# Attention with block means of v: loading the means' blocks in halves and earlier, and summing the second batch's two steps later

## The chip, the cores and the metric

One core of a Trainium2 chip. The metric is the time of one execution on the device in microseconds (us). Three executions of the kernel before gave 515.78, 517.11 and 518.01 us; the median, 517.11, is what the changed kernel is compared with.

The core has TensorE (PE, with its weight loads PEld), VectorE (DVE), ScalarE (ACT), GpSimd (POOL) and SyncE (SP). Each works through its own instructions in order and waits on semaphores for the others. In this kernel every DMA is issued by SP, in one order, and all of them run on the same 16 DMA engines.

## The reference

```
block, window = (32, 16)
k_sum = k.reshape(B, H, nb, block, D).max(axis=3)
v_sum = v.reshape(B, H, nb, block, D).mean(axis=3)
scores_l = scale * q @ k.T                # kept where |i - j| < window
scores_s = scale * q @ k_sum.T + log(block)
a = softmax(concat[scores_l masked, scores_s])
x = a @ concat[v, v_sum]                  # B=2, H=8, S=768, D=64
h = x @ w_in;  y = (h * cos(h)) @ w_out   # 1536 tokens, 512 -> 2048 -> 512
h2 = y @ w_in2                            # 512 -> 1024
out = layernorm(h2 * softmax(h2)) * g_ln @ w_out2
```

## The kernel before

Attention comes first and takes up to some 118 us; then two feed-forward blocks follow, in which TensorE multiplies without a break. The change is in attention only.

**Pairs and steps.** Heads are worked in pairs, two heads side by side on 128 partitions: 8 pairs, pairs 0 to 3 for batch 0 and 4 to 7 for batch 1. A pair is worked in 3 groups of 256 queries, so there are 24 groups. A written-out loop of steps (L592) is a pipeline over groups. In step s, in this order: TensorE computes the scores of group s+1 (`emit_s`, sps), transposes the weights of group s-4 (`emit_t`, aps) and multiplies them with v (group s-5, `emit_av`, ops); ScalarE takes the exponential of group s-1 (L508); VectorE sums group s-2 (L512) and adds the mask and finds the maxima of group s (L500, `emit_max`), which frees the score bank of group s for group s+2 (two banks); GpSimd subtracts the maxima (L503) and normalises group s-2 (L521); ScalarE copies the transposed weights (`emit_at`) and the product (`emit_x`). As no engine goes out of order, a wait in one step holds the next step's work on that engine.

**Keys and queries of a pair** are loaded (`load_k`, `load_q`), copied into one tile of both heads (`pair_k` on VectorE, `pair_q` on ScalarE), transposed on TensorE (`emit_k`, `emit_q`: 12 transposes, L431), then the block maxima of the keys are found on VectorE (`emit_ksum`, L443) and ScalarE builds the keys of all windows and the scaled queries (`emit_kx`, `emit_qx`). In most pairs that is spread over the three steps of the pair before.

**Means of v.** A batch's v is loaded once more in blocks of 32 rows (`load_vb`, the tile vb: 96 partitions, one per pair and block, with both heads' 32 rows; four DMAs, one per pair, into 24 partitions each). `sum_v` sums head 0 on VectorE in one instruction (L405) and head 1 on GpSimd as a tree of five (L409, L412). `scale_v` divides on ScalarE (L417), and `place_vsum` writes a pair's means by DMA beside the rows of v that `load_v` fetched (the tile vt, three buffers). Batch 0's blocks are asked for before the loop, behind pair 2's keys and queries, and summed in step 1; batch 1's are asked for in step 5 and summed in step 8.

**First weights.** From step 9 on the loop also loads blocks of the first feed-forward's weights (`raw`, 512 KB), two ahead, and converts and splits them: ScalarE rewrites both halves of the 64-bit words (`rebias`, L162, L163), VectorE joins them (`finish`, L170), one step later ScalarE rounds (L185) and GpSimd takes the rest (L186). Step 10 converts the first block, step 11 the second, step 13 the third. x is split likewise in steps 7, 10, 13 and 16 (L202, L203).

Of the kernel before, what the change touches and what calls it, by code (L numbers as in the profile page):

```python
# [17 lines left out]
BLOCK = 32  # L18
# [15 lines left out]
def fused_kernel(  # L34
# [299 lines left out]
    def attention():  # L334
        st = ExitStack()
        with st:
# [18 lines left out]
            def load_q(n):  # L355
                q_t[n] = load_heads(q, n, "qt")
# [19 lines left out]

            def load_v(n):
                b, hp = divmod(n, NP)
                t = io.tile([P, NT, 2, D], F32, tag="vt", name="vt", bufs=3)
                for j in range(2):  # L380
                    o = v[b, 2 * hp + j].offset
                    nc.sync.dma_start(
                        out=t[0:WIN, 1:NT - 1, j, :],
                        in_=bass.AP(v.tensor, o + (QT - BAND) * D, [[D, WIN], [QT * D, NT - 2], [1, D]]),
                    )
                    nc.sync.dma_start(
                        out=t[0:WIN, 0:NT:NT - 1, j, :],
                        in_=bass.AP(v.tensor, o, [[D, WIN], [(S - WIN) * D, 2], [1, D]]),
                    )
                v_t[n] = t  # L390
# [1 line left out]
            vb_t, vm_t = {}, {}  # L392

            def load_vb(b):
                t = io.tile([NP * NS, 2, BLOCK, D], F32, tag="vb", name="vb", bufs=1)
                for hp in range(NP):
                    nc.sync.dma_start(  # L397
                        out=t[hp * NS:(hp + 1) * NS],
                        in_=v[b, 2 * hp:2 * hp + 2].rearrange("h (n j) d -> n h (j d)", j=BLOCK))
                vb_t[b] = t  # L400

            def sum_v(b):
                t = vb_t.pop(b)
                m = io.tile([NP * NS, 2, D], F32, tag="vm", name="vm")
                nc.vector.tensor_reduce(  # L405
                    out=m[:, 0, :], in_=t[:, 0].rearrange("p j d -> p d j"), op=ALU.add, axis=AX.X)
                n = BLOCK // 2
                while n > 1:
                    nc.gpsimd.tensor_tensor(  # L409
                        out=t[:, 1, 0:n], in0=t[:, 1, 0:n], in1=t[:, 1, n:2 * n], op=ALU.add)  # L410
                    n //= 2
                nc.gpsimd.tensor_tensor(out=m[:, 1, :], in0=t[:, 1, 0], in1=t[:, 1, 1], op=ALU.add)  # L412
                vm_t[b] = m

            def scale_v(b):
# [151 lines left out]
            nc.sync.dma_start(out=mask.rearrange("p t k -> p (t k)"), in_=c_mask)  # L567
            load_k(1)
            load_q(1)
            load_k(2)  # L570
            load_q(2)
            load_vb(0)
            load_v(0)
            nc.gpsimd.memset(small, 0.0)
            warm_up(7)
            pair_k(0)
# [15 lines left out]
            for step in range(NGR + LA):  # L592
                n, g = divmod(step, GPP)
                summed = LN <= step < NGR + LN
                ahead = n + 1 if g == 0 and n + 1 < NPAIR else 0

                warm_up(IDLE[g] if step < min(FILL) else 0)
                fill(step)
# [3 lines left out]
                    emit_t(step - LT)  # L602
                if step >= LA:
                    emit_av(step - LA)
                if g == 2 and n + 2 < NPAIR:
                    emit_k(n + 2)
                    emit_q(n + 2)

                weights.split()
                if LX <= step < NGR + LX:  # L610
# [23 lines left out]
                for c in range(KC):  # L634
                    if step == XS[c]:
                        xs_of[0, c] = split_x(0, c, xs_a)
                if g == 1 and n + 2 < NPAIR:
                    pair_k(n + 2)
                    pair_q(n + 2)

                if g == 1 and n + 3 < NPAIR:
                    load_k(n + 3)
                    load_q(n + 3)
                if step == 1:
# [3 lines left out]
                    place_vsum(0)  # L648
                if g == 1 and n + 1 < NPAIR:
                    load_v(n + 1)  # L650
                if g == 2 and n + 1 < NPAIR:
                    if n + 1 == NP:
                        scale_v(1)
                    place_vsum(n + 1)
                if step == 5:
                    load_vb(1)
                if step == 8:
                    sum_v(1)

    with tc.manual_schedule():  # L660

# [260 lines left out]
```

## Time and profile before

| | us |
|---|---|
| median of three executions | 517.11 |
| profiled execution, its own time | 517.66 |
| its span, first to last instruction | 515.8 |
| TensorE busy in the span | 480.3 |
| VectorE | 309.8 |
| ScalarE | 275.0 |
| GpSimd | 155.4 |

The profile is of one execution. Shares of busy time are means over stages: TensorE is busy for 93% of the span, but almost all of its idle time lies in the attention stage. So the stage is read by the timeline (instructions in order of time, each with the idle time of its engine before it and what ended that), the table of stretches and the chain of waits. The granted clock is a share of TensorE's full speed.

### The profile page before, as it was taken

The numbers are of one execution on the slowest core, as the hardware profiler recorded it, in microseconds if no ns is written. First come the engines' busy times: TensorE is split into PE (matmuls) and PEld (weight loads), VectorE is DVE, ScalarE is ACT, GpSimd is POOL, SyncE is SP. The second block draws the span as 40 slices with busy tenths as digits, with TensorE's granted clock in tenths as the row PEclk, the third lists the DMA queues.
The fourth block names the chain that finished last, engine by engine and source line by source line (L and its number), as shares of the span: only waits on it lengthen the run. The fifth ranks groups of instructions, "written<-read, shape, count | busy, mean of one in ns | idle before, by whom it ended". The sixth has DMA issues, their size and how long they took to land.

```text
span 515.8 us, 7574 instructions
## 1 busy us (share of the span) xinstructions
PE 480.3 (93%) x2818; PEld 393.1 (76%) x2818; DVE 309.8 (60%) x684; ACT 275.0 (53%) x504; POOL 155.4 (30%) x147
## 2 busy tenths in 40 slices
PE   7378679899999999999999999999999999999997
PEld 4266567677888888888888888888887888888887
DVE  2486888796444546465565655646577755665561
ACT  3356698864758666566565563787422223222221
POOL 0386889752423223222222230254103102110000
PEclk9859799999999999999999999999999999999999
DMA  8798976600132332322322321220000000000001
GB/s 245 163 221 197 273 209 194 179 4 0 43 122 83 92 113 82 110 95 81 116 89 88 117 83 38 85 83 1 1 0 22 20 22 20 22 20 22 35 26 43
DMA packets 44516, 44.57 MB, mean 86 GB/s; under 512 B 21440, under 2 KB 36416, under 8 KB 44096
## 3 DMA queue, kind: packets, MB, share of 16 engines
q1 hardware_dynamic: 44480, 44.09, 29.0%
q8 instruction: 22, 0.36, 0.3%
q14 instruction: 14, 0.11, 0.1%
HBM read 39.76 MB, written 3.15 MB: 83 GB/s over the span
## 4 chain that ended last, share of the span: by engine, by line
PE 74%; DMA 6%; DVE 6%; ACT 5%; POOL 4%; SPq 3%; issue 2%; POOLq 0%; DVEq 0%; ACTq 0%
PE y L275 25%; PE h L233 23%; PE o L799 12%; PE h L721 11%; DMA vb<-in_v_dram 5%; PE tp L769 2%; DMA qt<-in_q_dram 1%; POOL vb L409 1%; POOL sm L521 1%; POOL sm L503 1%; DMA raw<-in_moe_w_in_dram 1%; DVE vm L405 1%; SPq L397 1%; ACT raw L162 1%; SPq L423 1%
## 5 line engine op out<-in xcount | busy, mean ns | idle before, releaser
L233 PE MATMUL h<-xs,w 128*128 128x512 f32 x576 | 141.5, 392 | 1.1 <-ACT qx L475 1.1
L275 PE MATMUL y<-gs,w 128*128 128x512 f32 x576 | 138.2, 389 | 0.0
L275 PEld LDWEIGHTS y<-gs,w 128*128 128x128 f32 x576 | 108.0, 188 | 22.5
L233 PEld LDWEIGHTS h<-xs,w 128*128 128x128 f32 x576 | 107.1, 188 | 23.6 <-ACT qx L475 1.3
L186 POOL TENSOR_TENSOR w<-s,w 128x512 fp32r<-128x512 f32 x48 | 62.1, 1295 | 161.2 <-ACT w L185 139.8
L242 ACT ACTIVATE r<-h 128x512 int32<-128x512 f32 x48 | 28.6, 596 | 86.1 <-PE h L233 86.1
L247 DVE SCALAR_TENSOR_TENSOR r<-r,h 128x512 f32<-128x512 int32 x48 | 32.9, 686 | 67.1 <-ACT r L242 67.0
L799 PE MATMUL o<-w,ls 128*128 128x512 f32 (+1 forms) x312 | 67.8, 374 | 1.4 <-DVE ls L773 1.4
L721 PE MATMUL h<-w,xs 128*128 128x512 f32 x288 | 68.6, 393 | 0.0
L170 DVE SCALAR_TENSOR_TENSOR s<-raw 128x512 int32<-128x512 int32 x48 | 37.0, 770 | 48.0 <-ACT raw L163 40.6
L799 PEld LDWEIGHTS o<-w,ls 128*128 128x128 f32 x312 | 55.3, 188 | 12.1 <-DVE ls L773 1.9
L721 PEld LDWEIGHTS h<-w,xs 128*128 128x128 f32 x288 | 53.3, 188 | 10.7
L489 PE MATMUL sps<-kx,qx 64*64 64x120 f32 x384 | 28.2, 292 | 22.6 <-DVE ss L516 10.8
L738 ACT ACTIVATE e<-h,st 128x1024 f32<-128x1024 f32 (+1 forms) x13 | 13.6, 1050 | 64.3 <-DVE st L734 60.7
L489 PEld LDWEIGHTS sps<-kx,qx 64*64 64x64 f32 x384 | 22.3, 147 | 28.4 <-issue 12.8
L756 POOL TENSOR_TENSOR st<-st,mhalf 128x1 f32<-128x1 f32 x12 | 6.6, 550 | 118.1 <-DVE st L755 105.9
L203 POOL TENSOR_TENSOR xs<-X,xs 128x512 fp32r<-128x512 f32 x22 | 28.7, 1313 | 30.0 <-ACT xs L202 30.0
L252 ACT ACTIVATE r<-r,half_pi 128x512 f32<-128x512 f32 x48 | 34.4, 717 | 1.3 <-DVE r L247 1.3
L263 DVE TENSOR_TENSOR gs<-h,gs 128x512 fp32r<-128x512 f32 x48 | 32.6, 680 | 4.1 <-ACT gs L262 3.8
L257 DVE TENSOR_TENSOR h<-h,r 128x512 f32<-128x512 f32 x48 | 32.9, 685 | 0.4 <-ACT r L252 0.4
L163 ACT ACTIVATE raw<-raw 128x512 int32<-128x512 uint32 x48 | 31.9, 665 | 0.0
L162 ACT ACTIVATE raw<-raw 128x512 f32<-128x512 f32 x48 | 31.9, 664 | 0.0
(73 smaller groups left out, 547.2 us busy)
## 6 DMA issues: line engine op xcount, KB each, us to landing
raw<-in_moe_w_in_dram SPq DMA_DIRECT2D x24, 512.0 KB, 3.4
raw<-in_moe_w_out_dram SPq DMA_DIRECT2D x24, 512.0 KB, 4.4
vt<-in_v_dram SPq DMA_DIRECT2D x16, 240.0 KB, 6.5
kt<-in_k_dram SPq DMA_DIRECT2D x8, 384.0 KB, 7.5
qt<-in_q_dram SPq DMA_DIRECT2D x8, 384.0 KB, 7.3
vb<-in_v_dram SPq DMA_DIRECT2D x8, 384.0 KB
out_dram<-osb SPq DMA_DIRECT2D x11, 256.0 KB, 2.1
vt<-vm SPq DMA_DIRECT2D x8, 144.0 KB
```

The source lines that it names most:

```text
L162: nc.scalar.activation(out=hw, in_=hw, func=AF.Prelu, scale=REBIAS, alpha=NEGATIVE)
L170: nc.vector.scalar_tensor_tensor(out=self.f32[i], in0=t[:, :, 1], scalar=3, in1=t[:, :, 0], op0=ALU.logical_shift_left, op1=ALU.bitwise_or)
L186: nc.gpsimd.tensor_tensor(out=w[:, 1, :], in0=f, in1=as32(w[:, 0, :]), op=ALU.subtract)
L233: nc.tensor.matmul(h, lhsT=w[:, a, f * P:(f + 1) * P], rhs=xs_of[tb, c][:, b_, :], start=(m == 0), stop=(m == 3 * KC - 1))
L247: nc.vector.scalar_tensor_tensor(out=r, in0=r.bitcast(I32), scalar=TWO_PI, in1=h_of[step], op0=ALU.mult, op1=ALU.subtract)
L252: nc.scalar.activation(out=r, in_=r, func=AF.Sin, scale=-1.0, bias=half_pi)
L257: nc.vector.tensor_tensor(out=h, in0=h, in1=r, op=ALU.mult)
L263: nc.vector.tensor_tensor(out=gs[:, 1, :], in0=r, in1=as32(gs[:, 0, :]), op=ALU.subtract)
L275: nc.tensor.matmul(y[e], lhsT=w[:, a, e * P:(e + 1) * P], rhs=gs[:, b_, :], start=(f == 0 and i == 0), stop=(f == GF - 1 and i == 2))
L489: nc.tensor.matmul(sps[h, i, :], lhsT=qx[h, t * QT:(t + 1) * QT], rhs=kx[h, t, :], start=True, stop=True)
L721: nc.tensor.matmul(banks[n], lhsT=xs_of[NTB + t // TPB, c][:, a, t0:t0 + P], rhs=weights.done[w2i[c][n]][:, b_, :], start=(m == 0), stop=( ...
L799: nc.tensor.matmul(o, lhsT=ls_of[t][f // 4][:, a, s0:s0 + P], rhs=w[:, b_, cols], start=(f == 0 and i == 0), stop=(f == NF2 - 1 and i == 2))
```

## The change

Five edits, all in the attention stage.

- `load_vb` fetches a pair's blocks in two halves of 16 rows: eight DMAs of 192 KB in place of four of 384 KB, into the same 24 partitions per pair. In `sum_v` VectorE's sum goes over two axes in place of one, and the tree's first addition adds the halves; sizes and counts stay.
- Before the loop, batch 0's blocks and pair 0's v are asked for ahead of pair 2's keys and queries.
- Pair 2's copies go from step 1 to step 2, its transposes from step 2 to step 3, its block maxima, kx and qx from step 3 to step 4; pair 3's loads go from step 1 to step 2.
- Batch 1's sum goes from step 8 to step 10, its scaling and the first placing from step 11 to step 12.
- v has four buffers in place of three.

```
-                t = io.tile([P, NT, 2, D], F32, tag="vt", name="vt", bufs=3)
+                t = io.tile([P, NT, 2, D], F32, tag="vt", name="vt", bufs=4)
...
-                    nc.sync.dma_start(
-                        out=t[hp * NS:(hp + 1) * NS],
-                        in_=v[b, 2 * hp:2 * hp + 2].rearrange("h (n j) d -> n h (j d)", j=BLOCK))
+                    src = v[b, 2 * hp:2 * hp + 2].rearrange("h (n a j) d -> n h a (j d)", a=2, j=BLOCK // 2)
+                    for a in range(2):
+                        nc.sync.dma_start(
+                            out=t[hp * NS:(hp + 1) * NS, a].rearrange("n h j d -> n h (j d)"), in_=src[:, :, a])
...
-                    out=m[:, 0, :], in_=t[:, 0].rearrange("p j d -> p d j"), op=ALU.add, axis=AX.X)
+                    out=m[:, 0, :], in_=t[:, :, 0].rearrange("p a j d -> p d a j"), op=ALU.add, axis=AX.XY)
+                nc.gpsimd.tensor_tensor(out=t[:, 0, 1], in0=t[:, 0, 1], in1=t[:, 1, 1], op=ALU.add)
...
             load_q(1)
+            load_vb(0)
+            load_v(0)
             load_k(2)
             load_q(2)
-            load_vb(0)
-            load_v(0)
...
-                ahead = n + 1 if g == 0 and n + 1 < NPAIR else 0
+                ahead = n + 1 if g == int(n == 1) and n + 1 < NPAIR else 0
...
-                if g == 2 and n + 2 < NPAIR:
-                    emit_k(n + 2)
-                    emit_q(n + 2)
+                if step == 3 or g == 2 and 0 < n < NPAIR - 2:
+                    emit_k((step + 4) // GPP)
+                    emit_q((step + 4) // GPP)
...
-                if g == 1 and n + 2 < NPAIR:
+                if g == (1 if n else 2) and n + 2 < NPAIR:
                     pair_k(n + 2)
                     pair_q(n + 2)
...
-                if step == 8:
+                if step == 10:
                     sum_v(1)
+                if step == 12:
+                    scale_v(1)
+                    place_vsum(NP)
```

SP's row of DMAs before the loop and in its first steps, before (kt and qt are keys and queries, vb the blocks, vt the rows of v):

```order
L350 DMA kt<-in_k_dram 128x6x128
L350 DMA qt<-in_q_dram 128x6x128
L397 DMA vb<-in_v_dram 24x2x2048 x4
L382 DMA vt<-in_v_dram 96x10x64
L386 DMA vt<-in_v_dram 96x2x64
L382 DMA vt<-in_v_dram 96x10x64
L386 DMA vt<-in_v_dram 96x2x64
L350 DMA kt<-in_k_dram 128x6x128
L350 DMA qt<-in_q_dram 128x6x128
L382 DMA vt<-in_v_dram 96x10x64
```

and now:

```order
L399 DMA vb<-in_v_dram 24x2x1024 x8
L382 DMA vt<-in_v_dram 96x10x64
L386 DMA vt<-in_v_dram 96x2x64
L382 DMA vt<-in_v_dram 96x10x64
L386 DMA vt<-in_v_dram 96x2x64
L350 DMA kt<-in_k_dram 128x6x128
L350 DMA qt<-in_q_dram 128x6x128
L382 DMA vt<-in_v_dram 96x10x64
L386 DMA vt<-in_v_dram 96x2x64
L382 DMA vt<-in_v_dram 96x10x64
L386 DMA vt<-in_v_dram 96x2x64
L350 DMA kt<-in_k_dram 128x6x128
```

The eight half loads and v of pair 0 stand ahead of pair 2's kt and qt, and v of pair 1 ahead of pair 3's.

TensorE's row from the first scores (sps) on, with the transposes of keys and queries (qk), before:

```order
L431 MATMUL qk<-ident,qg 128x128 x6
L489 MATMUL sps<-kx,qx 64x120 x24
L431 MATMUL qk<-ident,kg 128x128 x6
L431 MATMUL qk<-ident,qg 128x128 x6
L489 MATMUL sps<-kx,qx 64x120 x16
L528 MATMUL aps<-ident,sm 120x128 x4
L489 MATMUL sps<-kx,qx 64x120 x8
L528 MATMUL aps<-ident,sm 120x128 x4
L546 MATMUL ops<-at,vt 64x64 x8
L431 MATMUL qk<-ident,kg 128x128 x6
```

and now:

```order
L434 MATMUL qk<-ident,qg 128x128 x6
L492 MATMUL sps<-kx,qx 64x120 x32
L434 MATMUL qk<-ident,kg 128x128 x6
L434 MATMUL qk<-ident,qg 128x128 x6
L492 MATMUL sps<-kx,qx 64x120 x8
L531 MATMUL aps<-ident,sm 120x128 x4
L492 MATMUL sps<-kx,qx 64x120 x8
L531 MATMUL aps<-ident,sm 120x128 x4
L549 MATMUL ops<-at,vt 64x64 x8
L434 MATMUL qk<-ident,kg 128x128 x6
```

Eight rows of scores are one group, so x24 are groups 1 to 3 and x32 groups 1 to 4: pair 2's transposes (the qk rows behind them) stand one group later.

GpSimd's row around batch 1's tree (vb, vm), with the splits of x (xs) and of the weights (w), before:

```order
L521 TENSOR_TENSOR sm<-sm,ss 128x480
L409 TENSOR_TENSOR vb<-vb 96x1024
L409 TENSOR_TENSOR vb<-vb 96x512
L409 TENSOR_TENSOR vb<-vb 96x256
L409 TENSOR_TENSOR vb<-vb 96x128
L412 TENSOR_TENSOR vm<-vb 96x64
L503 TENSOR_TENSOR sm<-sm,mx 128x480
L521 TENSOR_TENSOR sm<-sm,ss 128x480
L503 TENSOR_TENSOR sm<-sm,mx 128x480
L521 TENSOR_TENSOR sm<-sm,ss 128x480
L203 TENSOR_TENSOR xs<-X,xs 128x512
L186 TENSOR_TENSOR w<-s,w 128x512
```

and now:

```order
L524 TENSOR_TENSOR sm<-sm,ss 128x480
L506 TENSOR_TENSOR sm<-sm,mx 128x480
L524 TENSOR_TENSOR sm<-sm,ss 128x480
L203 TENSOR_TENSOR xs<-X,xs 128x512
L409 TENSOR_TENSOR vb<-vb 96x1024
L412 TENSOR_TENSOR vb<-vb 96x512
L412 TENSOR_TENSOR vb<-vb 96x256
L412 TENSOR_TENSOR vb<-vb 96x128
L415 TENSOR_TENSOR vm<-vb 96x64
L186 TENSOR_TENSOR w<-s,w 128x512
L506 TENSOR_TENSOR sm<-sm,mx 128x480
```

The tree stood in step 8; now it stands in step 10, behind that step's split of x and right ahead of the first split of weights, which the subtraction of step 11 (L506, L503 before) follows.

## Rows read from the trace of the kernel before

**Rows 1.** stretches: us, busy (count) of PE, PEld, DVE, ACT, POOL; clock, DMA share, GB/s

```profile
18.44:28.60 10.16, 0.00 (x1) 0.03 (x1) 5.10 (x12) 0.00 (x0) 4.79 (x4) 0.72 0.85 202
...
49.62:56.70 7.08, 0.00 (x0) 0.00 (x0) 5.91 (x12) 1.25 (x3) 5.10 (x5) 0.78 0.87 230
...
117.80:515.80 398.00, 393.51 (x1816) 326.90 (x1816) 226.13 (x376) 199.23 (x360) 82.06 (x70) 1.00 0.17 57
```

**Rows 2.** timeline, first stall: start us, us, engine, line, operation, names, shapes [idle before <-releaser]

```profile
23.46 3.63 DVE L405 TENSOR_REDUCE vm<-vb 96x64 f32<-96x2048 f32 x1 [7.64 <-DMA vb<-in_v_dram]
...
23.50 5.03 POOL L409 TENSOR_TENSOR vb<-vb 96x1024 f32<-96x1024 f32 x4 [6.83 <-DMA vb<-in_v_dram]
...
28.60 1.86 PE L489 MATMUL sps<-kx,qx 64*64 64x120 f32 x16 [10.16 <-DVE ss L516]
...
28.61 0.32 POOL L412 TENSOR_TENSOR vm<-vb 96x64 f32<-96x64 f32 x1
...
28.96 0.31 ACT L417 ACTIVATE vm<-vm 96x128 f32<-96x128 f32 x1 [11.37 <-POOL vm L412]
...
29.29 2.15 SPq L423 DMA_DIRECT2D vt<-vm  x2
```

**Rows 3.** the chain of work to 75 us: start us, us, what

```profile
10.68 12.66 DMA vb<-in_v_dram
...
39.23 11.37 DMA vb<-in_v_dram
```

**Rows 4.** timeline, second stall, the columns of rows 2

```profile
50.79 3.63 DVE L405 TENSOR_REDUCE vm<-vb 96x64 f32<-96x2048 f32 x1 [3.80 <-DMA vb<-in_v_dram]
...
53.65 1.64 SPq L138 DMA_DIRECT2D raw<-in_moe_w_in_dram  x3
...
56.70 1.86 PE L489 MATMUL sps<-kx,qx 64*64 64x120 f32 x16 [7.09 <-DVE mx L500]
```

**Rows 5.** DMA in stretches of 2 us, the columns of rows 1

```profile
8.00:10.00 2.00, 1.55 (x15) 0.96 (x14) 1.40 (x3) 1.17 (x3) 0.00 (x0) 1.00 1.13 333
...
14.00:16.00 2.00, 1.09 (x18) 0.89 (x18) 1.83 (x13) 2.00 (x5) 1.57 (x2) 1.00 0.87 160
...
40.00:42.00 2.00, 2.00 (x37) 1.60 (x36) 1.97 (x17) 1.54 (x3) 1.22 (x2) 1.00 0.81 164
```

**Rows 6.** timeline, steps 10 to 13, the columns of rows 2

```profile
58.53 0.69 ACT L162 ACTIVATE raw<-raw 128x512 f32<-128x512 f32 x1
...
59.80 0.69 DVE L170 SCALAR_TENSOR_TENSOR s<-raw 128x512 int32<-128x512 int32 x1 [1.06 <-ACT raw L163]
...
60.73 1.15 POOL L521 TENSOR_TENSOR sm<-sm,ss 128x480 f32<-128x480 f32 x1 [1.06 <-DVE ss L520]
...
63.08 1.28 POOL L186 TENSOR_TENSOR w<-s,w 128x512 fp32r<-128x512 f32 x1
...
64.32 0.98 POOL L503 TENSOR_TENSOR sm<-sm,mx 128x480 f32<-128x480 f32 x1
...
65.06 0.31 ACT L417 ACTIVATE vm<-vm 96x128 f32<-96x128 f32 x1
...
66.42 0.59 ACT L508 ACTIVATE sm<-sm 128x480 f32<-128x480 f32 x1
...
69.83 0.64 ACT L508 ACTIVATE sm<-sm 128x480 f32<-128x480 f32 x1
...
71.60 0.69 DVE L170 SCALAR_TENSOR_TENSOR s<-raw 128x512 int32<-128x512 int32 x1 [1.35 <-ACT raw L163]
```

**Rows 7.** page, part 6, DMA issues: count, KB each, median us to landing

```profile
raw<-in_moe_w_in_dram SPq DMA_DIRECT2D x24, 512.0 KB, 3.4
raw<-in_moe_w_out_dram SPq DMA_DIRECT2D x24, 512.0 KB, 4.4
```

**Rows 8.** what the DMA queue (SP) waited for: us in total, times, longest

```profile
SPq L382 <- PE ops L546: 20.9, 5, 6.6
```

**Rows 9.** timeline, the transposes of pair 3's keys, the columns of rows 2

```profile
37.29 0.87 PE L431 MATMUL qk<-ident,kg 128*128 128x128 f32 x6
```

More of the change, by code (lines that the diff above doesn't have):

```diff
@@ L394, in load_vb @@
             def load_vb(b):
-                t = io.tile([NP * NS, 2, BLOCK, D], F32, tag="vb", name="vb", bufs=1)
+                t = io.tile([NP * NS, 2, 2, BLOCK // 2, D], F32, tag="vb", name="vb", bufs=1)
                 for hp in range(NP):
-                    nc.sync.dma_start(
-                        out=t[hp * NS:(hp + 1) * NS],
-                        in_=v[b, 2 * hp:2 * hp + 2].rearrange("h (n j) d -> n h (j d)", j=BLOCK))
+                    src = v[b, 2 * hp:2 * hp + 2].rearrange("h (n a j) d -> n h a (j d)", a=2, j=BLOCK // 2)
+                    for a in range(2):
+                        nc.sync.dma_start(
+                            out=t[hp * NS:(hp + 1) * NS, a].rearrange("n h j d -> n h (j d)"), in_=src[:, :, a])
                 vb_t[b] = t
@@ L405, in sum_v @@
                 nc.vector.tensor_reduce(
-                    out=m[:, 0, :], in_=t[:, 0].rearrange("p j d -> p d j"), op=ALU.add, axis=AX.X)
-                n = BLOCK // 2
+                    out=m[:, 0, :], in_=t[:, :, 0].rearrange("p a j d -> p d a j"), op=ALU.add, axis=AX.XY)
+                nc.gpsimd.tensor_tensor(out=t[:, 0, 1], in0=t[:, 0, 1], in1=t[:, 1, 1], op=ALU.add)
+                n = BLOCK // 4
                 while n > 1:
                     nc.gpsimd.tensor_tensor(
-                        out=t[:, 1, 0:n], in0=t[:, 1, 0:n], in1=t[:, 1, n:2 * n], op=ALU.add)
+                        out=t[:, 0, 1, 0:n], in0=t[:, 0, 1, 0:n], in1=t[:, 0, 1, n:2 * n], op=ALU.add)
                     n //= 2
-                nc.gpsimd.tensor_tensor(out=m[:, 1, :], in0=t[:, 1, 0], in1=t[:, 1, 1], op=ALU.add)
+                nc.gpsimd.tensor_tensor(out=m[:, 1, :], in0=t[:, 0, 1, 0], in1=t[:, 0, 1, 1], op=ALU.add)
                 vm_t[b] = m
@@ L636, in attention @@
                         xs_of[0, c] = split_x(0, c, xs_a)
-                if g == 1 and n + 2 < NPAIR:
+                if g == (1 if n else 2) and n + 2 < NPAIR:
                     pair_k(n + 2)
                     pair_q(n + 2)
-                if g == 1 and n + 3 < NPAIR:
+                if g == (1 if n else 2) and n + 3 < NPAIR:
                     load_k(n + 3)
@@ L650, in attention @@
                     load_v(n + 1)
-                if g == 2 and n + 1 < NPAIR:
-                    if n + 1 == NP:
-                        scale_v(1)
+                if g == 2 and n + 1 < NPAIR and n + 1 != NP:
                     place_vsum(n + 1)
```

## The prediction

> **What bounds the kernel now.** I read the stretches first. From 117.80 us on TensorE is busy 393.51 of 398.00 us at the full clock [rows 1]; no edit touches that part, so it only moves with the end of the attention stage. In front of it lie two stretches in which TensorE does nothing: 10.16 us up to 28.60 and 7.08 us up to 56.70 [rows 1]. The timeline names the cause: in both, VectorE's sum of v's blocks (3.63 us, starting at 23.46 and 50.79) stands ahead of the maxima that free the score banks, and TensorE's scores start only after it [rows 2, 4]. The chain of waits says what that sum waited for: the four loads of vb, landed at 10.68 + 12.66 = 23.34 us, and those of the second batch, at 39.23 + 11.37 = 50.60 us [rows 3]. So what both stalls hang on is the stream of loads, and the question is what a load becomes late for when another goes ahead of it. Behind 56.70 the steps are a ring of ScalarE, VectorE and GpSimd work: exponentials, conversion of the first weights, normalising, splitting [rows 6]. A delay inside that ring goes on to the end.
>
> **What the trace says of vb's rate.** At 8 to 10 us, when keys and queries are loaded, the queue moves 333 GB/s; at 14 to 16 us, in vb's first loads, 160, and at 40 to 42, in the second ones, 164 [rows 5]. Four loads of 384 KB are 1.57 MB; at 160 GB/s that is 9.8 us. Does a load in halves move faster? The rows show no half block, so I bound it: not at all (9.8 us) or at the keys' rate (1.57 MB / 333 GB/s = 4.7 us). I take 9.8, because whole and half blocks go into the same 24 partitions per load, and both stretches of whole blocks show one rate whatever ran beside them.
> The Trainium skill ("SBUF — State Buffer", Door 1: The DMA port swizzle) says that the rate of a DMA goes by how many of the 16 ports its partitions reach, four neighbouring partitions to a port; 24 partitions reach 6 ports, and 6/16 of its 435 GB/s is 163 GB/s, an estimate from that page. The trace agrees with 160 and 164. By that rule halves change nothing, and the sum stays; without it vb would be 5.1 us shorter, the case of the first rival.
>
> **First batch's vb ahead of pair 2's k and q.** Two loads of 384 KB (786 KB) no longer stand ahead of it. At 333 GB/s that is 2.4 us; at the stall's mean of 202 GB/s [rows 1] it would be 3.9. I take 2.5, nearer to the first, since k and q move at the fast rate: landing at 20.8 in place of 23.34. Eight issues in place of four cost SyncE more time (three took 1.64 us [rows 4], so some 2.2 us for four more), hidden beside the 10 us of data that the queue then moves; without that cover it would be 2.2 us. VectorE's sum keeps its 2048 elements and 3.63 us, GpSimd's tree keeps its sizes, from 23.50 to 28.61 + 0.32, which is 5.43 us [rows 2].
>
> **Pair 2 a step later.** Its copies, its 12 transposes and the building of its keys (kx, qx) go behind the stall. Before, the transposes ran ahead of it, free. Now they stand between the scores on TensorE, and the scores of step 5 wait for keys that ScalarE builds in step 4, behind that step's copy of the transposed weights: the slack of one step is gone. I followed steps 2 to 6 with the durations of the trace: pair 3's transposes, at 37.29 before [rows 9], come out within half a microsecond of that, so what the first stall gives up the steps spend again. The sum below doesn't hang on it, since step 10 waits for its weights either way with some 4 us in hand. What remains of the 2.5 us is that the queue runs earlier: the first mean of v is scaled at 28.96 and placed from 29.29 [rows 2], now 2.5 us sooner, and all loads behind that with it. Two loads more (pair 3's) are now issued ahead of the placing, as the order above shows: 0 to 1.1 us, at 0.55 an issue.
>
> **Second batch's sum two steps later.** vb's second loads land at 50.60 - 2.5 = 48.1 or later; the sum stands at the end of step 10, and the wait of 3.80 us at step 8 is gone from its place. Steps 9 and 10 now run ahead of the sum, and what they need next is late: step 10 converts the first weight block. Its load, the first of three issued from 53.65 [rows 4], stands behind the second vb and v of pair 3 in the queue. Moved by 2.5 us less 0 to 1.1 it is issued at 51.2 to 52.3; I take 51.4, since SyncE then still waits for the scaled means most of that time. The two kinds of weight loads land 3.4 and 4.4 us after issue in the median [rows 7]: 54.6 to 56.7, taken as 55.3 (the middle, 3.9 after 51.4). Before, ScalarE read that block at 58.53 without waiting for it [rows 6]: vb's stall had covered the load. Now ScalarE waits for it, with the conversion on VectorE behind it, and the sum and the tree behind that.
> From there, on rows 6. Conversion on VectorE: 59.80 - 58.53 = 1.27 us after ScalarE's start, so 56.6 (before 59.80). GpSimd then normalises, splits x and splits the weight block until it subtracts step 11's maxima; 64.32 - 59.80 = 4.52 us after the conversion's start, now with the tree between: 56.6 + 4.52 + 5.43 = 66.55, 2.2 later than before. Step 11's exponential waits for that (0.98 us): 67.55 for 66.42, 1.1 later. To step 12's exponential ScalarE has 69.83 - 66.42 = 3.41 us, and now also the scaling of the means, 0.31, which stood a step earlier [rows 6]: 71.3, 1.45 later. The third block's conversion (71.60 before [rows 6]) follows it by the same 1.45. The tree also meets a conversion on VectorE that reads two SBUF inputs; either may wait for the other, 0 to 0.69 us (one conversion), taken as 0.3.
> Sum: +1.75 us, of which I take 1.7; from +0.7 (weights at 54.6, no clash) to +3.5 (56.7 and a full clash), and -0.7 where vb gains the 3.9 us above.
>
> **Four v buffers.** SyncE waited 20.9 us in 5 pieces for the product with v to give a buffer back [rows 8]. These waits end. The first of them, before pair 3's v, is followed by issues that wait on room in the queue behind vb anyway; the later ones load v for a pair two or more steps ahead. I cost it at nothing; with more gained, the weights come up to 1 us sooner, which is inside the range.
>
> **Rivals.** (a) Halves move at the keys' rate. Then both vb's are 5.1 us shorter, the weights land by 46, ahead of use. Step 8 is through on VectorE at 50.79 - 3.80 = 46.99 [rows 4]; steps 9 and 10 took from 54.42 (the sum's end) to 59.80, 5.38 us, so the conversion starts at 52.4. With 4.52 + 5.43 step 11's subtraction comes at 62.3, 2.0 earlier than before, its exponential 3.0 and step 12's 2.7 earlier. The first stall also ends 5.1 us sooner, of which I count half, since the steps spend some of it: -5.2, which gives 511.9. For it speaks only that it was not measured; against it one rate in both stretches.
> (b) Slower: the queue gains nothing beyond the two extra issues and the tree clashes. The point is the weight block landing at 56.2: there the end is 2.6 us later. At 56.7 and a full clash it is 3.5 later: 520.6. For it: 1.1 us of issues and the slower landing median of 4.4 us give just that. Against: the first kind of weight load, which this one is, has the median of 3.4.
> (c) The change does not bring vb earlier: each load waits for the completion of the load eight issues back (the order shows one of eight counters before each), so eight small pieces hang on pair 1's loads, and v and pair 2's keys on the pieces. If vb still lands at 23.34, the weights land at 53.65 + 3.9 = 57.6, and the end is 1.7 + 2.3 = 4.0 later: 521.1. Against it: pair 1's loads and those ahead of them are 1.96 MB, 6 us at 333 GB/s, so in by 10 us, while vb's last piece is only due to move near 19.
>
> **How the numbers follow.** The profiled execution took 517.66 us, 0.55 above the median of 517.11; 517.66 + 1.7 = 519.4, on the median's scale 518.8. Half a per cent is 2.6 us, about what a measurement can tell from no change. Chances: forecast (no change beyond 2.6 us) 0.52, (b) 0.27, (a) 0.13, (c) 0.05, and 0.03 for a gain between (a) and the forecast. Faster 0.16, same 0.52, slower 0.32. The range goes from 514.0 (all but the most of (a)) to 521.3 ((c) and most of (b)); the forecast's own is 517.8 to 520.4.
>
> **What would show it.** In the changed kernel's trace: vb's sum starts near 20.9 and TensorE's first gap is some 2.5 us shorter; VectorE no longer waits for vb at step 8; ScalarE waits for the first weight block at step 10, up to about 55, and TensorE has a gap there; GpSimd's tree runs from about 60 to 65 and step 11's exponential comes at 67 to 68. I am wrong if the weights are there before step 10 asks for them, if vb's rate is above 200 GB/s, or if steps 11 to 13 have slack that takes the tree in.

## The result and the profile after

The changed kernel took 521.88 us in the median of 4 executions (520.55 to 521.90), the kernel before, beside it, 516.97 (515.78 to 518.01): a ratio of 1.0089, with an interval of 1.0062 to 1.0116. It is slower by 4.9 us. The prediction said 518.8 and a range up to 521.3; the time lies above the range. Measured again later on one chip with other kernels it was 521.31 to 516.46, 1.0096 (1.0069 to 1.0124).

The profiled execution took 520.55 us, 2.9 above that of before (517.66). I read it in the order of the prediction. The stretches (the columns of rows 1) answer to rows 1 and 5: the first gap of TensorE is 8.44 us where it was 10.16, the part behind attention is as long as before, and half blocks move at 158 and 168 GB/s in the two stretches shown (in stretches of 2 us from 34 to 38 us, where other loads run among them, the queue moves 138 to 203).

```profile
16.13:24.57 8.44, 0.01 (x1) 0.03 (x1) 5.11 (x12) 0.77 (x2) 4.81 (x5) 0.73 0.97 237
121.38:518.70 397.32, 392.94 (x1804) 326.45 (x1800) 225.36 (x375) 199.27 (x360) 82.07 (x70) 1.00 0.17 58
...
37.00:39.00 2.00, 2.00 (x22) 1.54 (x21) 0.00 (x0) 0.98 (x3) 0.00 (x0) 0.50 0.76 158
38.00:40.00 2.00, 2.00 (x19) 1.88 (x16) 0.00 (x0) 1.02 (x3) 0.00 (x0) 0.50 0.80 168
```

The timeline of the first batch (start us, us, engine, line, operation, names, shapes, idle before) answers to rows 2 and 9. The sum starts 4.0 us sooner than before and the scores too (24.57 for 28.60), but pair 3's transposes, 37.29 before, come at 38.50, and VectorE waits 4.57 us for them. Many of TensorE's rows here are long: six transposes take 1.54 us, in [rows 9] 0.87. And the copy of pair 2's keys (L368), done ahead of the stall before (0.76 us at 15.07), now stands right behind it and takes 2.55 us beside GpSimd's work: step 3's maxima come 8.23 us behind the start of the sum (27.66 - 19.43), before 6.63 (30.09 - 23.46). First the copy in the kernel before, then the rows of the changed one:

```profile
15.07 0.76 DVE L368 COPY kg<-kt 128x768 f32<-128x768 f32 x1
```

```profile
19.43 3.63 DVE L407 TENSOR_REDUCE vm<-vb 96x64 f32<-96x2048 f32 x1 [5.11 <-DMA vt<-in_v_dram]
...
24.57 1.87 PE L492 MATMUL sps<-kx,qx 64*64 64x120 f32 x16 [8.44 <-DVE ss L519]
...
24.64 2.55 DVE L368 COPY kg<-kt 128x768 f32<-128x768 f32 x1
...
27.24 1.54 PE L434 MATMUL qk<-ident,kg 128*128 128x128 f32 x6 [0.80 <-DVE kg L368]
...
34.61 1.86 PE L492 MATMUL sps<-kx,qx 64*64 64x120 f32 x16 [2.89 <-ACT qx L478]
...
38.50 1.54 PE L434 MATMUL qk<-ident,kg 128*128 128x128 f32 x6
...
41.02 0.96 DVE L446 TENSOR_REDUCE ksum<-qk 128x24 f32<-128x768 f32 x1 [4.57 <-PE qk L434]
```

The timeline of steps 10 to 13 answers to rows 4 and 6. VectorE no longer waits for vb: the sum stands behind the conversion (L170), the tree behind step 10's split of x. The first weight block is asked for at 49.98 (L138), and ScalarE starts on it (L162) at 55.01, right behind an exponential that ends at 54.93. Step 11's subtraction comes at 66.54, its exponential at 67.55, step 12's at 71.18.

```profile
49.98 1.64 SPq L138 DMA_DIRECT2D raw<-in_moe_w_in_dram  x3
...
54.33 0.60 ACT L511 ACTIVATE sm<-sm 128x480 f32<-128x480 f32 x1
...
55.01 0.67 ACT L162 ACTIVATE raw<-raw 128x512 f32<-128x512 f32 x1
...
56.24 0.69 DVE L170 SCALAR_TENSOR_TENSOR s<-raw 128x512 int32<-128x512 int32 x1 [2.67 <-ACT raw L163]
...
57.38 3.82 DVE L407 TENSOR_REDUCE vm<-vb 96x64 f32<-96x2048 f32 x1
...
59.51 2.37 POOL L409 TENSOR_TENSOR vb<-vb 96x1024 f32<-96x1024 f32 x1
...
65.04 0.32 POOL L415 TENSOR_TENSOR vm<-vb 96x64 f32<-96x64 f32 x1
...
66.06 4.61 DVE L519 TENSOR_SCALAR ss<-ss 128x4 f32<-128x4 f32 x1
...
66.54 0.98 POOL L506 TENSOR_TENSOR sm<-sm,mx 128x480 f32<-128x480 f32 x1
...
67.55 0.60 ACT L511 ACTIVATE sm<-sm 128x480 f32<-128x480 f32 x1 [3.05 <-POOL sm L506]
...
71.18 0.61 ACT L511 ACTIVATE sm<-sm 128x480 f32<-128x480 f32 x1
...
72.92 0.99 DVE L170 SCALAR_TENSOR_TENSOR s<-raw 128x512 int32<-128x512 int32 x1 [0.61 <-ACT raw L163]
```

SP's wait for a v buffer, 20.9 us in [rows 8], is all but gone:

```profile
SPq L382 <- PE ops L549: 1.0, 2, 0.8
```

**Where the time went.** I followed each group's exponential through both traces. Step 9's comes 3.7 us sooner than before, step 11's 1.1 later and step 12's 1.35 (forecast 1.1 and 1.45), step 14's 1.61 later; step 15's is 3.00 later, and the rows behind it stay about that late. Between steps 14 and 15 another 1.4 us appear that the prediction did not have. In front of them stand two rows out of the ordinary: a small addition on VectorE (L519, four numbers a row) that takes 4.61 us and not 0.19, and a run of TensorE at half clock from 68 to 78 us, where the kernel before had the full one (the expectations below write 68.7 to 78.5; read again it is 67.8 to 78.0). The chain of waits in this trace names both: it runs over the addition, and over TensorE from 72.37 to 87.44. Rows of TensorE there, the first four 1.6 to 1.8 times as long as with the filler further down:

```profile
72.37 1.87 PE L492 MATMUL sps<-kx,qx 64*64 64x120 f32 x16 [1.45 <-DVE ss L519]
74.17 1.11 PE L531 MATMUL aps<-ident,sm 128*120 128x128 f32 x4
75.20 1.12 PE L549 MATMUL ops<-at,vt 120*64 120x64 f32 x16
76.26 1.54 PE L434 MATMUL qk<-ident,kg 128*128 128x128 f32 x6
...
78.40 0.94 PE L233 MATMUL h<-xs,w 128*128 128x512 f32 x3
```

So three questions went to the chip. Is it the later sum that costs, or the first batch's edits (theories A and B)? Is the jump behind step 14 the half clock or the blocked addition (C and D)? And what holds the conversion in step 10, from which all else follows (E to H)?

### The profile page after: what moved, and what is told of

It reads as the page before. It is cut to its first block, busy times and chain, and to the rows that moved or that the text cites. A ratio compares the mean times of both kernels' runs of the same rounds, so it can differ in the third digit from the quotient of the medians.

```text
span 518.7 us, 7588 instructions
## 1 busy us (share of the span) xinstructions
PE 484.0 (93%) x2818; PEld 396.3 (76%) x2818; DVE 315.3 (61%) x684; ACT 275.6 (53%) x504; POOL 155.6 (30%) x147
## 4 chain that ended last, share of the span: by engine, by line
PE 75%; DVE 9%; DMA 6%; SPq 4%; ACT 2%; issue 1%; POOL 1%; DVEq 0%; ACTq 0%
PE y L275 25%; PE h L233 24%; PE o L804 12%; PE h L726 11%; DMA vb<-in_v_dram 2%; DMA vt<-in_v_dram 2%; SPq L386 2%; PE tp L774 2%; DVE vm L407 1%; DVE ss L519 1%; DMA raw<-in_moe_w_in_dram 1%; PE sps L492 1%; DVE sm L503 1%; PE ops L549 1%; SPq L350 1%
## 5 line engine op out<-in xcount | busy, mean ns | idle before, releaser
L804 PE MATMUL o<-w,ls 128*128 128x512 f32 (+1 forms) x312 | 67.8, 374 | 1.4 <-DVE ls L778 1.4
L170 DVE SCALAR_TENSOR_TENSOR s<-raw 128x512 int32<-128x512 int32 x48 | 36.7, 764 | 48.6 <-ACT raw L163 41.6
L185 ACT ACTIVATE w<-s 128x512 fp32r<-128x512 f32 x48 | 30.1, 627 | 5.0 <-DVE s L170 4.8
L162 ACT ACTIVATE raw<-raw 128x512 f32<-128x512 f32 x48 | 31.9, 664 | 0.1
```

Source lines behind the costliest of these rows:

```text
L162: nc.scalar.activation(out=hw, in_=hw, func=AF.Prelu, scale=REBIAS, alpha=NEGATIVE)
L170: nc.vector.scalar_tensor_tensor(out=self.f32[i], in0=t[:, :, 1], scalar=3, in1=t[:, :, 0], op0=ALU.logical_shift_left, op1=ALU.bitwise_or)
L804: nc.tensor.matmul(o, lhsT=ls_of[t][f // 4][:, a, s0:s0 + P], rhs=w[:, b_, cols], start=(f == 0 and i == 0), stop=(f == NF2 - 1 and i == 2))
```

## Which edit costs

**The sum back in step 8**, all else of the change kept:

```
-                if step == 10:
+                if step == 8:
                     sum_v(1)
```

with scaling and first placing back in step 11.

> The changed kernel with batch 1's sum back in step 8 and its scaling and first placing back in step 11; halves, early loads, pair 2's move and four buffers stay. Theory A (the later sum is the whole loss): vb's second loads land at 47.1 as in the changed kernel, ahead of the 49.2 at which VectorE asks for them (46.99 + 2.2), so nothing waits; step 9's maxima come at about 54.1 (55.76 before), the first weights, landed by 55.0, are not waited for, and the end is 1.6 us earlier than before: 515.4, that is 6 us below the changed kernel. Theory B (the early loads and pair 2's later step lose as well, since step 6 came 2.2 us late): the end is not earlier than before: 517 to 519.

Measured: 516.90 us in the median, before 516.65, ratio 1.0002 (0.9983 to 1.0021). Its profiled execution, 515.99, is the fastest of its twelve. In it the sum starts without a wait to speak of, as A said, and the lag of step 15 is -1.62:

```profile
49.16 3.72 DVE L407 TENSOR_REDUCE vm<-vb 96x64 f32<-96x2048 f32 x1 [0.20 <-DMA qt<-in_q_dram]
```

By the median A's gain of 1.6 us is not there: halves, early loads, pair 2's move and the fourth buffer make no difference in sum. Theory B's time, 517, holds: something eats what the vanished wait gives (the stretch from vb's sum to step 6, below).

**The sum in step 10 alone**, in the kernel before (sum, scaling and placing as in the change's last piece, nothing else).

> The kernel before with only batch 1's sum in step 10, its scaling and first placing in step 12. Theory A: the first weights are issued only at 53.6 and land at 57.1, step 10's conversion starts at 58.4 and not at 59.8, the tree follows it on GpSimd, step 11's subtraction comes at 68.3 (64.32 before): slower than before by 3 to 4 us, 520 to 521. Theory B: the move alone costs under 1 us: 517 to 518.

Measured: 522.64 us, ratio 1.0105 (1.0076 to 1.0134): 6.0 us slower, more than A's 3 to 4. ScalarE waits 6.77 us for the weights, the conversion stands where it stood before (59.77 for 59.80), and the sum and the tree behind it push step 12's exponential to 74.69, 4.86 later than before:

```profile
58.55 0.65 ACT L162 ACTIVATE raw<-raw 128x512 f32<-128x512 f32 x1 [6.77 <-DMA raw<-in_moe_w_in_dram]
59.77 0.69 DVE L170 SCALAR_TENSOR_TENSOR s<-raw 128x512 int32<-128x512 int32 x1 [9.37 <-ACT raw L163]
...
63.04 5.44 POOL L409 TENSOR_TENSOR vb<-vb 96x1024 f32<-96x1024 f32 x4
...
74.69 0.60 ACT L508 ACTIVATE sm<-sm 128x480 f32<-128x480 f32 x1
```

So the move of the sum is the loss. The other edits make no difference by themselves; that they give back about 1 us of it (522.64 for 521.88 and 521.31) is not shown, as the intervals overlap.

**The sum in step 9**, one step later than before (the same edit with 9).

> The changed kernel with batch 1's sum in step 9, one step later than before and one earlier than in the change; scaling and first placing in step 11 as before. Theory E: VectorE sums and GpSimd runs the tree in the time in which step 10 waits for the weights anyway; the tree is over by 58.4, the conversion at 57.6 is not held, step 11's subtraction comes at 62.1 (64.32 before): 515 to 516, the best so far. If the sum costs its 3.63 and 5.43 us wherever it stands behind step 8, it is slower than before by 2 us or more: 519.

Measured: 517.70 us, ratio 1.0020 (1.0002 to 1.0039). That is 4.2 us below the changed kernel, between the two expectations: in step 9 the sum lies beside the wait for the weights for the most part. It is 0.8 above the sum in step 8, within the intervals, so it is not shown to be faster or slower than that. Its profiled execution is the slowest of twelve, so I take nothing finer from it.

## The jump behind step 14

**Filler on TensorE.** `warm_up(n)` multiplies a constant tile n times into a bank that nobody reads.

```
-                warm_up(IDLE[g] if step < min(FILL) else 0)
+                warm_up({12: 13, 13: 5, 14: 6}.get(step, 0))
...
                     emit_s(step + 1)
+                warm_up({13: 6}.get(step, 0))
```

> The changed kernel with idle products on TensorE (13 ahead of step 12's scores, 5 ahead of step 13's, 6 behind them, 6 ahead of step 14's; 0.21 us each), in the gaps of 59.5 to 72.4 us; no other work is touched. Theory C (the half clock from 68.7 to 78.5 costs: it stretches TensorE's run from step 14's scores on by 2.6 us): the clock stays full there and the end is 1.4 us earlier than in the changed kernel, since ScalarE's chain, 1.6 us behind the kernel before, then sets it. Theory D (only VectorE's small addition of 4.61 us at 66.06 costs): the clock stays full and the time is the changed kernel's, within 0.3 us.

Measured: 520.53 us (ratio 1.0067, 1.0041 to 1.0093), 1.35 below the changed kernel's 521.88 and 0.8 below its second median; the intervals overlap, so the trace has to decide. The granted clock from 66 to 76 us (the columns of rows 1, clock third from the end) is 0.59 in the changed kernel, the first line, and 1.00 with filler, the second:

```profile
66.00:76.00 10.00, 6.80 (x70) 5.47 (x72) 9.36 (x27) 8.45 (x18) 8.48 (x9) 0.59 0.30 82
```

```profile
66.00:76.00 10.00, 8.67 (x99) 5.26 (x97) 9.33 (x25) 6.03 (x13) 9.02 (x11) 1.00 0.17 58
```

The rows of TensorE that answer to those above, in the kernel with filler:

```profile
75.43 1.04 PE L492 MATMUL sps<-kx,qx 64*64 64x120 f32 x16 [0.95 <-DVE ss L519]
76.59 0.62 PE L531 MATMUL aps<-ident,sm 128*120 128x128 f32 x4
77.14 0.69 PE L549 MATMUL ops<-at,vt 120*64 120x64 f32 x16
77.76 0.88 PE L434 MATMUL qk<-ident,kg 128*128 128x128 f32 x6
...
79.04 0.94 PE L233 MATMUL h<-xs,w 128*128 128x512 f32 x3
```

From the scores to the product h it is 3.61 us (79.04 - 75.43) where the changed kernel takes 6.03. And the jump is gone: the lag to the kernel before is 4.68 us at step 14's exponential and 4.68 at step 15's. The addition still takes 4.62 us in this run. (That the lag is large in this profile comes from a conversion at 59.28; more on that below.)

**Without the addition** of 1e-9 in step 12:

```
-                if summed:
+                if summed and step - LN != 10:
                     emit_guard(step - LN)
```

> The changed kernel without one instruction: the addition of 1e-9 to group 10's sums in step 12 (the one that took 4.61 us at 66.06) is left out. Theory D: VectorE goes on at once, step 13's maxima come 2 to 4 us earlier than 71.33 and the end 1.4 us or more earlier. Theory C alone (half clock): the end moves by under 0.4 us. If both stand in series on TensorE, either this or the filler takes the 1.4 us, down to ScalarE's chain. If the reciprocal behind it is held in its place (4 us instead of 0.18), nothing moves and the addition itself was not at fault but the port it shares.

Measured: 521.52 us, ratio 1.0093 (1.0066 to 1.0120). VectorE does go on at once: step 13's maxima, 15.09 us behind the conversion in the changed kernel (71.33 - 56.24), come 12.52 behind it (70.09 - 57.57). Yet the clock is half, the rows of TensorE are as long as in the changed kernel, and the lag still jumps, from 2.66 us at step 14's exponential to 3.91 at step 15's:

```profile
70.09 0.27 DVE L503 CUSTOM_DVE_ANT_0 sm<-sps,mask 128x120 f32<-128x120 f32 x1
...
70.90 2.99 DVE L519 TENSOR_SCALAR ss<-ss 128x4 f32<-128x4 f32 x1
```

```profile
72.52 1.86 PE L492 MATMUL sps<-kx,qx 64*64 64x120 f32 x16 [0.27 <-ACT qx L478]
...
76.92 1.54 PE L434 MATMUL qk<-ident,kg 128*128 128x128 f32 x6
```

This run alone doesn't clear the addition, since part of the wait only moved: the same addition of the next step, at 70.90, now takes 2.99 us. But there it holds no row of TensorE: the scores at 72.52 wait for ScalarE's qx. And in the run with filler the addition takes its 4.62 us while the jump is gone. With the two together theory D falls, and so does "either of the two takes it": the most striking row of the trace, 4.61 us for four numbers and a piece of the chain of waits, costs nothing that these runs can see. The jump is the half clock (C).

## What holds the conversion

In eight profiles with the sum in step 10 I read the start of step 10's conversion (C) and of step 12's exponential. The distance is the same to 0.05 us in all of them, whatever else was changed, 4.9 us more than before:

| profiled execution | C | step 12's exponential | distance | time | time - C | half clock behind step 12 |
|---|---|---|---|---|---|---|
| before | 59.80 | 69.83 | 10.03 | 517.66 | 457.86 | no |
| the change | 56.24 | 71.18 | 14.94 | 520.55 | 464.31 | yes |
| the change again | 56.04 | 70.97 | 14.93 | 519.85 | 463.81 | yes |
| without the addition | 57.57 | 72.52 | 14.95 | 521.77 | 464.20 | yes |
| weights first | 57.18 | 72.12 | 14.94 | 521.00 | 463.82 | yes |
| sum in step 10 alone | 59.77 | 74.69 | 14.92 | 523.30 | 463.53 | yes |
| filler, steps 12 to 14 | 59.28 | 74.25 | 14.97 | 522.25 | 462.97 | no |
| filler everywhere | 56.64 | 71.61 | 14.97 | 519.62 | 462.98 | no |
| filler and weights first | 53.63 | 68.58 | 14.95 | 516.62 | 462.99 | no |

The time of an execution is C, plus 463.0, plus 0.5 to 1.3 us where TensorE runs at half clock behind step 12. The kernel before has 457.9 there: the sum behind the conversion costs 5.1 us and must be earned by a conversion that comes earlier. What keeps it from coming earlier?

**The first weight block asked for in step 5**, ahead of batch 1's blocks:

```
                 if step == 5:
+                    weights.load(0)
                     load_vb(1)
```

> The changed kernel with the load of the first weight block asked for in step 5, right ahead of batch 1's blocks, in place of step 9; nothing else is touched. In three profiles the conversion came 1.25 us after that block had landed (54.98, 56.32 and 58.03), and the end followed the conversion. Theory E (the landing sets the conversion): ScalarE is free at 54.9, the conversion comes at 56.2 in every run, and the median falls by 1.3 us from 521.9 to 520.6. Theory F (ScalarE and VectorE are not free sooner, the wait is only a resting place): no change, 521.5 to 522.

Measured: 521.34 us, ratio 1.0074 (1.0045 to 1.0103). The time doesn't decide: by the medians the gain is 0.5 us at most, by the ratios (1.0074 for 1.0089 and 1.0096) about 1, and the intervals overlap. The trace does, against E: the conversion is at 57.18 and not at 56.2. The weights are there long before, but ScalarE isn't: it starts on them where its exponential ends, at 56.0.

```profile
55.44 0.61 ACT L511 ACTIVATE sm<-sm 128x480 f32<-128x480 f32 x1
...
55.92 0.69 ACT L162 ACTIVATE raw<-raw 128x512 f32<-128x512 f32 x1
...
57.18 0.69 DVE L170 SCALAR_TENSOR_TENSOR s<-raw 128x512 int32<-128x512 int32 x1 [2.51 <-ACT raw L163]
```

So two floors lie under the conversion, both near 55 to 56: the weights' landing, and the steps themselves. That the steps are so late goes back to the first batch. From the start of vb's sum to step 6's maxima the kernel before takes 16.27 us (23.46 to 39.73), the changed one 22.47 (19.43 to 41.90), and what the sum wins is lost again there. TensorE ran at half clock in most of that stretch, and 1.6 us of the 6.2 stand at step 3's maxima already, behind the copy of 2.55 us.

**Filler in all gaps of TensorE**, and **the same with the weights first**: two runs that lift the second floor alone, and both.

```
+                warm_up({3: 33, 5: 10, 11: 8, 12: 13, 13: 5, 14: 6}.get(step, 0))
...
                     emit_s(step + 1)
+                warm_up({3: 6, 13: 6}.get(step, 0))
```

> The changed kernel (sum in step 10) with idle products on TensorE in all its gaps: 33 ahead of step 3's scores and 6 behind them, 10 ahead of step 5's, 8 ahead of step 11's, and those of the run with filler in steps 12 to 14. Theory G (two floors under step 10's conversion: the first weights' landing, 56.3 in a usual run, and ScalarE's own steps, free at 56.0 since pair 2's transposes ran at half clock): the filler lifts only the second; the landing still sets the conversion, so the time is that of the run with filler in steps 12 to 14: 520.5, above the kernel before by 3.5 to 4.5. Theory H (the late step 6 is what costs): 517 to 518.

Measured: 520.22 us, ratio 1.0086 (1.0058 to 1.0113). As G said: the steps are early now (vb's sum at 19.04, step 6's maxima at 37.45, 18.41 us behind it), the exponential is through at 50.5, and ScalarE waits 4.93 us for the weights.

```profile
49.88 0.62 ACT L511 ACTIVATE sm<-sm 128x480 f32<-128x480 f32 x1
55.42 0.65 ACT L162 ACTIVATE raw<-raw 128x512 f32<-128x512 f32 x1 [4.93 <-DMA raw<-in_moe_w_in_dram]
56.64 0.69 DVE L170 SCALAR_TENSOR_TENSOR s<-raw 128x512 int32<-128x512 int32 x1 [7.53 <-ACT raw L163]
```

> The same filler, and the first weight block asked for in step 5 as in the run with the weights first. Theory G: with both floors lifted the conversion comes at 52.5 to 53.5 and not at 57.2, and the end 3 to 4 us earlier than with the filler alone: 516.5 to 517.5, though the sum still stands in step 10. If the sum in step 10 costs its time in any case, 519.5 to 520.5.

Measured: 515.51 us, ratio 0.9983 (0.9965 to 1.0001), 1 us below the range that G gave. With both floors lifted the conversion is at 53.63 in a profile whose first loads were late (vb's sum at 21.06), and the kernel with the sum in step 10 is 4.7 us faster than with filler alone and 5.8 faster than with the weights first alone. Either floor alone hides what the other is worth.

```profile
52.37 0.68 ACT L162 ACTIVATE raw<-raw 128x512 f32<-128x512 f32 x1
...
53.63 0.69 DVE L170 SCALAR_TENSOR_TENSOR s<-raw 128x512 int32<-128x512 int32 x1 [2.51 <-ACT raw L163]
```

**Filler with the sum in step 9, and in the kernel before.** Four counts in the first case (`{3: 33, 5: 10, 11: 12}` ahead of the scores, `{3: 6}` behind), two in the second (`{3: 40, 10: 28}`).

> The kernel of the sum in step 9 with idle products on TensorE in the first gap (33 ahead of step 3's scores, 6 behind them), ahead of step 5's scores (10) and of step 11's (12). Theory C: TensorE is at full clock from 20 to 41 us, pair 2's transposes take 0.9 in place of 1.5 us and step 6 comes 1 to 1.5 us sooner; the end gains that only if the sum, not the weights, sets step 10: 0 to 1.2 us below the kernel without filler. If the clock there costs nothing, the same time within 0.3 us.

Measured: 515.86 us, ratio 0.9976 (0.9955 to 0.9998), against 1.0020 (1.0002 to 1.0039) without filler; the gain of 1.8 us is above the 0 to 1.2 expected. The clock from 18 to 41 us is 1.00 (first line), without filler 0.65 from 18 to 42 (second):

```profile
18.00:41.00 23.00, 20.90 (x209) 13.57 (x206) 19.58 (x72) 10.60 (x20) 15.55 (x16) 1.00 0.99 244
```

```profile
18.00:42.00 24.00, 11.90 (x95) 9.58 (x92) 15.37 (x49) 8.08 (x15) 13.11 (x13) 0.65 0.90 222
```

> The kernel before with idle products on TensorE in its two gaps (40 ahead of step 3's scores, 28 ahead of step 10's). Theory C: the clock stays full from 23 to 37 and from 54 to 61 us, but behind both gaps GpSimd, ScalarE and the loads set the pace, not TensorE: the time stays within 0.5 us of 516.7. If the half clock costs wherever it falls, as it does behind step 13 of the changed kernel, the time falls by 1.3 us or more.

Measured: 517.01 us, ratio 1.0001 (0.9984 to 1.0018): no difference, as C expected. From vb's sum to step 6's maxima filler takes 2.3 us off the kernel before too (13.99 for 16.27), but there step 8 waits for vb's second loads, and most of the time won ends in that wait (5.53 us for 3.80). Behind the second gap the filler did not hold the clock (0.73 from 54.6 to 61 us), so the run tests the first gap alone. In these runs the half clock costs only where TensorE's work is what the next step waits for.

**Sum in step 9, filler, weights first.**

> The kernel with the sum in step 9 and filler (515.9), and the first weight block asked for in step 5. There ScalarE waited 2.8 us for that block; GpSimd's tree, over at 54.1, stands beside that wait. Theory G: the conversion comes earlier, but the tree is then what step 10 waits for: 0.3 to 1.5 us less, 514.5 to 515.5. If vb's second loads, now behind the block, come too late for step 9, the time is not lower: 516 to 517.

Measured: 515.33 us, ratio 0.9994 (0.9968 to 1.0020), executions from 513.34 to 520.21. The spread is too wide to set it above or below the two kernels at 515.5 and 515.9. In its profiled execution, one of the slower ones (517.48), a load holds the sum of step 9, and the sum holds the conversion: ScalarE is on the weights at 52.46, but VectorE is in the sum until 55.95 and converts at 57.30. Whether that is so in the faster executions stays open.

```profile
52.16 3.79 DVE L407 TENSOR_REDUCE vm<-vb 96x64 f32<-96x2048 f32 x1 [2.78 <-DMA kt<-in_k_dram]
```

> The changed kernel itself, beside the others on one chip. It took 521.9 us in the median and 520.55 in the profiled execution. Every theory expects 521 to 522; its profile shows whether the conversion at 56.24 of the first profile was early (landing 54.98) against a usual run (56.3 expected, and conversion at 57.6).

Measured: 521.31 us, ratio 1.0096; its profiled execution, 519.85, has the conversion at 56.04, straight behind an exponential from 54.30: there the steps were the floor, and the weights' landing, that I expected to see, was not.

## Why the prediction failed

**Right.** Halves move at the old rate, 158 to 168 GB/s; rival (a) falls. The ring of steps 10 to 13 came out nearly as forecast: the conversion at 56.24 (forecast 56.6), step 11's subtraction at 66.54 (66.55), its exponential at 67.55 (67.55), step 12's at 71.18 (71.3), the third block's conversion 1.32 later than before (1.45). VectorE's wait in step 8 is gone. With four buffers SP's waits for one are all but gone, and no run shows a gain from it.

**In part luck.** That the ring's times are so near comes from misses that cancel. The first weight block was asked for at 49.98 and not at 51.4, and ScalarE read it 5.0 us after that and not 3.9. ScalarE hardly waited for it: its own steps were over at 54.93, so the conversion would have come at about 56.1 without any load (an estimate from the second profile of the changed kernel, where it comes at 56.04 behind an exponential from 54.30, here from 54.33). And from the conversion to step 11's subtraction it took 10.30 us for 9.95, which makes up for a conversion 0.36 earlier.

Two steps failed: what the earlier conversion earns was taken 1.7 to 2.2 us too high, and the clock of TensorE, 0.8 to 1.3 us, was left out. Together they are the 3.1 us between forecast and result.

**The step that failed: "Sum: +1.75 us", taken from step 12's exponential straight to the end.** The sum follows ScalarE, VectorE and GpSimd. TensorE is not in it: the prediction names its gap in step 10 as a sign, and doesn't ask at what clock TensorE comes back. Here it idled for 3.08 us up to 62.61 and 1.34 up to 66.19, and twice more behind, was granted half clock from 68 on, and its rows became the path. From step 14's exponential to step 15's that costs 1.4 us in the first profile of the changed kernel, 0.9 in the second, and nothing with filler.

**Mis-sized: what the earlier conversion earns, 3.2 us.** The prediction set one execution of the changed kernel against one of before. By the table an execution of before at the median, 516.97, would have its conversion at 59.1 (516.97 - 457.86), and one of the changed kernel at 521.88 at 57.6 or 58.1 (less 464.31 or 463.81, its two profiles): estimates, since no trace of such a pair exists. The gain is then 1.0 to 1.5 us. With the 5.1 for the sum behind it and 0.8 to 1.3 for the clock that is the +4.9 measured. That the profiled executions lay on opposite sides of their medians (before 0.7 above it, the change 1.3 below) made the two traces look nearer than the kernels are; the 0.55 that the prediction allowed for it was on one side only.

**"The sum doesn't hang on it", of pair 2's later step.** This was the reason given for not following steps 2 to 6 further, "with some 4 us in hand". There was nothing in hand. Pair 3's transposes came not within half a microsecond of 37.29 but 1.2 later, step 6's maxima 2.2 later, although vb's sum started 4.0 sooner and not 2.5. (In eleven profiles with the change's first loads it started between 19.04 and 21.51, 20.23 in the mean, in three with those of before between 21.83 and 23.46, 22.73 in the mean: 2.5 was right as a usual value, and the 4.0 comes from the two executions that were set side by side.) The steps reached the conversion at the same moment as the weights. The stretch from the sum to step 6's maxima grew by 6.2 us, 16.27 to 22.47. With filler it is 13.99 in the kernel before and 18.41 in the changed one: 4.4 of the 6.2 are pair 2's moved step and the order around it, and the half clock takes 4.1 in place of 2.3, which is the other 1.8. Of the 4.4, 1.6 stand at step 3's maxima, with filler or without, behind the copy of pair 2's keys that takes 2.55 us (2.47 with filler) beside GpSimd: the prediction moved that copy without asking which engine would be at work beside it. No run takes the copy out, so its share is argued. The clock is the same omission as above at another place: the scores behind the gap took 1.86 us in [rows 2], and I did not ask why.

**The clash, 0.3 us, at most 0.69.** The tree took 5.85 us for 5.43, 0.4 more. But a small addition waited 4.61 us, far beyond the bound, and that cost nothing that shows.

**Rival (b)** had the direction and, at its bound, 520.6, a time 1.3 short, by a mechanism that holds in part: in two of four profiles of the same first twelve steps the weights came after 56 (56.34 without the addition, 58.06 with filler in steps 12 to 14). **Rival (c)**, 521.1, was nearest in time, for the wrong reason: vb did come earlier.

**What stays open.** Why the landings differ by 3 us from one execution to the next, which by the table is most of the spread of the times, was not tried. Most of it is there before the load begins: in the four profiles that are one program up to step 12 the first weight block is asked for at 49.02, 49.98, 50.59 and 53.86. Nor was the fourth buffer alone, or halves alone; together with the early loads they come to nothing.

## What to carry to other kernels

Work that is moved behind a wait costs its full price from there on, and earns only what the wait gets shorter: look for every floor under the step that waits (the load, and each engine's own way to it), since lifting one of two equal floors shows nothing. When a change opens a gap on TensorE, price the rows behind the gap at half clock and ask whether they are on the path; idle products in the gap are a cheap test and here part of a version that is 0.2% faster than the kernel before, just clear of noise (sum in step 9 with filler, 0.9976, 0.9955 to 0.9998). And read a distance between two kernels from a quantity that is constant over executions, as the time less the conversion here, not from the two executions that happened to be profiled.

## What the runs showed of the hardware

**An addition of four numbers a row waited through five instructions of GpSimd, but others like it did not.** At 66.06 VectorE began L519, which takes 0.17 us where GpSimd pauses (72.14, for one); it ended at 70.67, when the last of five instructions of GpSimd, one straight behind the other from 65.31, ended at 70.65. The same row took 4.59 to 4.62 us in the six other profiles with the sum in step 10 that had it. The Trainium skill ("SBUF — State Buffer", Who interferes with whom) says that a `tensor_scalar` on VectorE can, in some of its modes, use the ports that it shares with GpSimd, and that whoever comes first has them for the whole instruction while the other is blocked. The trace agrees that it is blocked and not slowed. But it gives no rule for how long: thirteen other L519 rows of the same trace that met GpSimd at work took 0.42 to 1.26 us, and ended as the one instruction that was running ended, though in all but one of these the next had begun without a pause. So it was at 75.73, where GpSimd went from one split to the next:

```profile
75.25 1.28 POOL L203 TENSOR_TENSOR xs<-X,xs 128x512 fp32r<-128x512 f32 x1
75.73 0.82 DVE L519 TENSOR_SCALAR ss<-ss 128x4 f32<-128x4 f32 x1
...
76.48 1.28 POOL L186 TENSOR_TENSOR w<-s,w 128x512 fp32r<-128x512 f32 x1
```

What decides between the two stays open.

**TensorE's clock.** In the changed kernel it stood at half (1.2 of 2.4 GHz) in most of 20 to 41 us and again from 68 to 78, in or behind a gap of 8.44 us the first time, behind gaps of 3.08 and 1.34 the second. Filler in the gaps kept it at 1.00 from 18 to 41 us in the one kernel and from 66 to 76 in the other. It took 4.1 us off the stretch from vb's sum to step 6 and the whole jump behind step 14; in the kernel before it took 2.3 off that stretch and nothing off the time, since a load ended last there (by the wait of 5.53 us in step 8).
